# New tables of order, engines and places for a linear-attention and two-MLP kernel

## The chip, the cores and the metric

The kernel runs on one core of a Trainium2 chip. The metric is device time in microseconds (us) of one execution. Five engines work side by side, each through its own queue in order: TensorE (PE, matmuls; PEld are its weight loads), VectorE (DVE), ScalarE (ACT), GpSimd (POOL) and SyncE (SP), which here issues all DMAs. An instruction that waits for another engine holds up everything behind it in its own queue.

## The reference

```python
# attention: batch 4, 8 heads, 576 rows, head_dim 64, 128 features
def phi(x):                      # x scaled by 64 ** -0.25
    proj = np.einsum('bhsd,md->bhsm', x, omega)
    h = proj - np.sum(x * x, axis=-1, keepdims=True) / 2.0
    return np.exp(h - np.max(h, axis=-1, keepdims=True)) / np.sqrt(m)
q_p, k_p = (phi(q_s), phi(k_s))
kv = np.einsum('bhsm,bhsd->bhmd', k_p, v)
num = np.einsum('bhsm,bhmd->bhsd', q_p, kv)
den = np.einsum('bhsm,bhm->bhs', q_p, np.sum(k_p, axis=2))[..., None] + 1e-06
attn = num / den                 # 2304 rows of 512 in all
# first MLP: 512 -> 2048 -> 512
h = np.maximum(x @ w_in, 0.0)
x = h * h @ w_out
# second MLP: rms norm, 512 -> 1536 (gate and value) -> 512
xn = x / np.sqrt(np.mean(x * x, axis=-1, keepdims=True) + 1e-06) * rms_g
g = xn @ w_gate
out = (g / (1.0 + np.exp(-g)) * (xn @ w_val)) @ w_out
```

## The kernel before, in words

The 2304 rows are worked in blocks: 512 rows of each of the four batches, and the 64 remaining rows of all four together as a fifth block of 256. The large matmuls run in float32r, with each operand split into a high part (a cast on ACT, L483) and a low part (a subtraction on DVE or POOL, L474) and three products of the parts. The small matmuls of the attention run in float32. Some block products of the first and second MLP are combined so that seven products replace eight, with sums of operands and results on DVE.

The stages overlap. Attention of a batch goes through pairs of heads. For a pair, PE makes the features of k and of q (L659, a block of 16 matmuls for 512 rows); DVE takes row sums of squares (L613, after a squaring at L580 to L582 on POOL, ACT or DVE), maxima (L666) and two small corrections (L671); ACT takes the exponential (L678); PE transposes (L772) and multiplies (L718, L778, remaining rows at L704, L721, L783); DVE divides (L753 to L757); PE turns the result (L817, L808), and ACT and DVE split it for the first MLP. The first MLP then works hidden unit by hidden unit: a hidden product (L893, 12 matmuls, all in the one PSUM bank of the class "h"), a relu (L908) and a square (L910) on ACT, a low part on DVE or POOL, and four output products of 3 matmuls (L924). The weights are decoded from their input format on DVE and ACT (L512 to L526) and split. The second MLP has products at L1202, sums of results at L1220, gating at L1379 and L1382 and output products at L1398, added up at L1406. In the first 54 us the attention of the first batch is done alone with the first decoded weights; until some 340 us attention is mixed with the first MLP.

Nothing of the order is left to a scheduler while the program is built. Each piece of work is a node with the engines that it may run on and the classes of buffers that it may use. The table ORDER lists all 3753 nodes in the order in which they are issued, and so sets the order in each engine's queue; its top four bits choose among a node's engines. PLACES says which buffer of which class each new buffer takes. The word ffff in ORDER stands for a filler: two matmuls of 256 columns on a tile of ones (L562), whose result nobody reads, issued on PE at that place. The reading of the tables is this:

```python
for w in words:
    if w == 0xFFFF:
        self.filler[1](filled)
        continue
    n = self.nodes[w & 0xFFF]
    n.eng, n.dur, n.fn = n.alts[w >> 12]
```

What a node waits for follows from its data and from the buffer that it takes: a buffer is taken again when its last reader is done.

Of the kernel before, what the change touches and what calls it, by code (L numbers as in the profile page):

```python
# [24 lines left out]
    "0000000400050007001400442045001500461016000300170009ffffffffffffffffffffffffffffffffffff0019000d000a"  # L25
    "0001001a001b0018001c001d00430020100b000c001f001e000e000f0021004f10220010ffffffff00240011002500260008"
    "004e007d001200230050007c00270013ffffffff00470028002affffffffffff0052004800490029004a004b002e002f0180"
    "002b0051002c003000530054004d007e004c0071ffff0080003100550183005601811182005800360037005c0072102d0042"
    "0191007f00810073008200d9003200830184009f00840059105d005a0057018501921193105b00750085005e0186003300da"
    "003400350086003801ae00760077007400640194007800790070005f00b8019501960065003900db1187ffff006000b90066"  # L30
    "006100670068003a00a00069007a003c01a1009e006200a300aa007b008a00ab008701a200a10197006300a41198003e01a4"
    "003b0088003f009201a300a500a200a600a7008c00e401af0089003d00e5008b11b00093013800ae01a510ac00ad0094008d"
    "00af00b000a900e600b100b2008e008f009500a801b100b400b3006b006e00ce00b5009600b600e7009700e80090009100ba"
    "01b201b300d8004000c000b7009901a600bb01be006f006a00bc00c100e900ea00c20041018900eb01a701b400ec00bd00be"
    "00bf009c006c00ee00c311b501c1018a00c400c500c700ca01bf00dd11c0009d00dc012e00cb018b006d00ed01c201c311a8"
    "00de10cf01da018c018d00cd00d000c60098009a01c400c800df00c900e0010400e101caffffffffffff0199019a01cb018e"
    "01cd01c501ce00e2019b019c0410118f01e700d101db11cc01cf0190019d01e811e901dc01dd110501de01b701b801b901df"
    "00d200d3009b01d011d1019e119f01ba01ac01e001a001e101ea01eb0157010f00d401f600d5020301aa00e301d301d401ec"
    "01f901f701ab11f801c600d601fa01ad01fb020401ed01ee010e111001bb21bc00cc01c8112f120502060207020801c70213"
    "01d201fc00f2022f00d701fd010601d501c900ef021f11bd01d601d721d801d901ef01f001f1021410f100f4011101390216"  # L40
    "023000f002170209021500f301b602180219023c01e30220012c01e4020a0200021a013000f50222022301e60102047100f6"
    "00f7020200f90221022400fa01e5023200f8024b011202310233023402250226023d0113011401f2020c020d01f301ff01f4"
    "0235020100fb0115020e113a023f01160240023e02410236011801f50117013b0103047202580107024e024f012d0274020f"
    "02420210010801881211024c02591243021d024d02280229025a025b01090250010a010b022a00fd021c0237021b0212025c"
    "025d025102520473022b0158026802840100010d0101021e0275127602770253025e0278027904061159022c010c02380244"
    "024502460247122d125f023a0285026b0269026c011c011d011e126a0119011a00fc0163026d0239015a0291011b00fe011f"
    "012001210122026e00ff0490122e0123023b116401650286126f027a027b0257013c013d013e02a002540255013f02870288"
    "01400256027c026102890124026201e2029402950292024801420125149124071249024a028a026302641293026501310296"
    "128b02bd02710492029701320133126601340135022702a301360267029801fe0270027d027e027f0141016202a112a2043c"
    "02a4027202a5028f02c002be12bf02c102ad01461148041d028002a612a702e602c2029901370260029a029b0273028e02ae"  # L50
    "02b012af02b102b2029c028102b302e7014302b602c902c312c40147014502b402d912e802b70144028d01a91282141e02ca"
    "02b80405041f0290040802cc02cd0283014902ac035202cb02ce035c014a029d129e02da014d03870156029f02dc02cf12d0"
    "014b014c014e02aa014f035d02db02a902f502ab02b902ba02dd02de12bb143d01660167035102df02c601270168016902d2"
    "02e9016a02ea012a02c502e0035e02d3016b02c702d10302012b02eb02bc02f802f9135302ec12ed015b015c030302f612f7"
    "031202e3015d016c02d4015e02d502fa015f03050306035402c8016004b702e402e202ee02ef02f0031302e102fb13040307"
    "028c035f0161131402f10170043e02b504c602f202e503500308031e02d603930171016d016e016f0368117212fc03090150"
    "015212d701530315031603170369032e030b033b015101540360015503210173030c017401770178017903180175017602d8"
    "030d1394030e0361017b22f3031f030102fe0388017e0362036302ff04b8017f0320136a030004b912f40364036503670355"
    "0322031904ba03230324031a031c030f13100366032f020b133004cb036b031d0331132503920356031b04bb03320357033e"
    "03580327032803290359035a033c02fd0447035b0395133d03330334033f017a037304d703400341017c017d032a032b132c"  # L60
    "030a0588131105861335036c036d036e033a036f037003710589033703740372032604bf03380339134203b204df04c00587"
# [1527 lines left out]
```

## Time and profile before

| | |
|---|---|
| median of 3 runs | 955.78 us (954.9 to 957.16) |
| profiled execution, own time | 957.46 us |
| its span, first to last instruction | 955.2 us |
| mean granted TensorE clock | 0.996 |
| busy: PE, DVE, ACT, POOL | 934.9, 743.2, 515.8, 108.2 us |

The profiled execution is 1.7 us above the median, and 2.3 us of its own time lie outside its span. A matmul's end is modelled in the profile, so PE is shown as busy for somewhat longer than it works; the distance from one matmul's start to the next one's is the better measure. In a dense stretch 12 matmuls of 512 columns take 2.72 us.

### The profile page before, as it was taken

The numbers are of one execution on the slowest core, as the hardware profiler recorded it, in microseconds if no ns is written. First come the engines' busy times: TensorE is split into PE (matmuls) and PEld (weight loads), VectorE is DVE, ScalarE is ACT, GpSimd is POOL, SyncE is SP. The second block draws the span as 40 slices with busy tenths as digits, with TensorE's granted clock in tenths as the row PEclk, the third lists the DMA queues.
The fourth block names the chain that finished last, engine by engine and source line by source line (L and its number), as shares of the span: only waits on it lengthen the run. The fifth ranks groups of instructions, "written<-read, shape, count | busy, mean of one in ns | idle before, by whom it ended". The sixth has DMA issues, their size and how long they took to land.

```text
span 955.2 us, 16357 instructions
## 1 busy us (share of the span) xinstructions
PE 934.9 (98%) x6062; PEld 780.7 (82%) x6062; DVE 743.2 (78%) x1354; ACT 515.8 (54%) x1077; POOL 108.2 (11%) x97
## 2 busy tenths in 40 slices
PE   8899999999999999999999999999999999999998
PEld 7777777878888888888889888888878888888886
DVE  6999999787676798887776778789998746655846
ACT  6888887735665477755345646455443333332321
POOL 2311222120302000010010011001110000101100
PEclk9999999999999999999999999999999999999999
DMA  8657889887978877778788553325232332212203
GB/s 275 222 199 262 286 276 338 292 265 255 325 264 265 276 239 248 239 259 288 243 305 286 196 150 109 113 75 156 77 100 82 100 106 67 67 56 63 72 21 111
DMA packets 78384, 182.10 MB, mean 191 GB/s; under 512 B 9184, under 2 KB 13408, under 8 KB 78304
## 3 DMA queue, kind: packets, MB, share of 16 engines
q1 hardware_dynamic: 78304, 181.06, 58.1%
q8 instruction: 48, 0.79, 0.3%
q14 instruction: 32, 0.26, 0.1%
HBM read 142.49 MB, written 38.54 MB: 190 GB/s over the span
## 4 chain that ended last, share of the span: by engine, by line
PE 79%; DVE 7%; ACT 2%; issue 1%; DMA 1%; SPq 0%; DVEq 0%; ACTq 0%
PE acc L1202 19%; PE t L1398 12%; PE t L1202 8%; PE acc L924 8%; PE h L893 7%; PE acc L1324 5%; PE h L1202 4%; PE t L1324 4%; PE h L1398 3%; PE t L659 2%; PE t L1304 2%; PE h L1304 1%; PE h L1324 1%; PE t L778 1%; DMA wq<-w2d0g 1%
## 5 line engine op out<-in xcount | busy, mean ns | idle before, releaser
L1202 PE MATMUL acc<-x,wq 128*128 128x512 f32 x439 | 153.1, 390 | 0.7 <-DVE cc L1220 0.7
L1202 PE MATMUL acc<-xa,wq 128*128 128x512 f32 x360 | 133.5, 390 | 0.0
L1220 DVE TENSOR_TENSOR cc<-acc,cc 128x512 f32<-128x512 f32 x115 | 78.4, 686 | 50.0 <-PE acc L1202 43.2
L1398 PE MATMUL t<-wq,ub 128*128 128x512 f32 x391 | 105.2, 389 | 0.0
L1202 PEld LDWEIGHTS acc<-x,wq 128*128 128x128 f32 x439 | 82.4, 188 | 18.4 <-DVE cc L1220 1.7
L483 ACT CAST wq<-wq 128x512 fp32r<-128x512 f32 x108 | 64.0, 618 | 60.6 <-DMA wq<-w2d3o 7.8
L474 DVE TENSOR_TENSOR wq<-wq 128x512 fp32r<-128x512 f32 x108 | 79.8, 752 | 17.6 <-ACT wq L483 17.5
L924 PE MATMUL acc<-g,wr 128*128 128x512 f32 (+1 forms) x396 | 91.2, 362 | 0.3 <-DVE g L474 0.2
L1398 PEld LDWEIGHTS t<-wq,ub 128*128 128x128 f32 x391 | 73.1, 188 | 15.1
L1202 PEld LDWEIGHTS acc<-xa,wq 128*128 128x128 f32 x360 | 67.4, 188 | 13.5
L678 ACT ACTIVATE p<-t,sm 128x128 f32<-128x128 f32 x212 | 60.1, 386 | 25.5 <-DVE sm L671 21.6
L924 PEld LDWEIGHTS acc<-g,wr 128*128 128x128 f32 x396 | 64.6, 189 | 11.2 <-issue 0.5
L893 PE MATMUL h<-x,wr 128*128 128x512 f32 x264 | 69.0, 398 | 1.1 <-ACT wr L483 0.5
L1406 DVE TENSOR_TENSOR oa<-t,oa 128x512 f32<-128x512 f32 x73 | 49.3, 684 | 18.6 <-PE t L1398 18.5
L893 PEld LDWEIGHTS h<-x,wr 128*128 128x128 f32 x264 | 48.3, 189 | 12.5 <-ACT wr L483 0.7
L666 DVE TENSOR_REDUCE sm<-t 128x4 f32<-128x512 f32 x59 | 38.5, 684 | 20.2 <-PE t L659 18.4
L521 ACT ACTIVATE dw<-st 128x512 f32<-128x512 f32 x59 | 40.4, 686 | 10.5 <-DMA st<-in_w_gate_dram 3.0
L1398 PE MATMUL t<-wq,g 128*128 128x512 f32 x143 | 45.1, 389 | 0.0
L526 DVE SCALAR_TENSOR_TENSOR dw<-dw,st 128x512 uint32<-128x512 uint32 x59 | 42.0, 715 | 3.1 <-ACT st L515 1.7
L483 ACT CAST ub<-cc 128x512 fp32r<-128x512 f32 x40 | 24.5, 620 | 34.3 <-DVE cc L1382 29.8
L924 PE MATMUL acc<-g,wu 128*128 128x512 f32 (+1 forms) x180 | 42.6, 362 | 0.0
L1202 PEld LDWEIGHTS t<-xq,wq 128*128 128x128 f32 x288 | 37.8, 191 | 2.0
(350 smaller groups left out, 1999.3 us busy)
## 6 DMA issues: line engine op xcount, KB each, us to landing
wr<-w1d SPq DMA_DIRECT2D x70, 512.0 KB, 5.7
st<-in_w_out_dram SPq DMA_DIRECT2D x28, 512.0 KB, 4.5
w1d<-wr SPq DMA_DIRECT2D x22, 512.0 KB, 6.0
st<-in_w_in_dram SPq DMA_DIRECT2D x16, 512.0 KB, 4.9
st<-in_w_gate_dram SPq DMA_DIRECT2D x12, 512.0 KB, 5.3
st<-in_w_val_dram SPq DMA_DIRECT2D x12, 512.0 KB, 5.7
st<-y SPq DMA_DIRECT2D x22, 256.0 KB, 3.7
v<-in_v_r_dram SPq DMA_DIRECT2D x16, 260.0 KB, 4.9
```

Source lines behind the costliest of these rows:

```text
L474: return lambda: en.tensor_tensor(out=lo(), in0=src(), in1=f32(hi()), op=ALU.subtract)
L483: first = plan.add("ACT", act(n), prio, lambda: nc.scalar.copy(out=hi(), in_=src()), rd, [whi], after, pre=[blo] if blo is not bhi else [])
L521: lambda: nc.scalar.activation(out=out(), in_=hf(), func=AF.Abs, scale=65536.0), [(st, 1)], [w])
L526: lambda: nc.vector.scalar_tensor_tensor(out=out().bitcast(U32), in0=out().bitcast(U32), scalar=3, in1=half(st.ap, 0), op0=ALU.logical_shi ...
L678: nc.scalar.activation(out=pbuf.ap[:, j, :], in_=fp.ap[:, i, :], func=AF.Exp, bias=mx.ap[:, j:j + 1])
L893: nc.tensor.matmul(hb.ap[:, :n], lhsT=u.ap[:, wl, kk * P:(kk + 1) * P], rhs=xcols(j, xl, kk)(), start=(gi == 0 and ii == 0), stop=(gi == l ...
L924: nc.tensor.matmul(accs[e].ap[:, :n], lhsT=u.ap[:, w, es], rhs=x.ap[:, :n], start=(c == 0 and i == 0), stop=(c == C1 - 1 and i == 2))
L1202: nc.tensor.matmul(bank.ap[:, cols], lhsT=u.ap[:, wl, c0 + kk * P:c0 + (kk + 1) * P], rhs=x[kk][xl].ap[:, :cols.stop - cols.start], start= ...
L1220: lambda: nc.vector.tensor_tensor(out=out.ap, in0=bank.ap, in1=x.ap, op=ALU.add), [bank, x], [out])
L1324: nc.tensor.matmul(bank.ap, lhsT=us[dc].ap[:, wl, es], rhs=gs[dc, j][xl].ap, start=dc == i == 0 and (j == 1 or first), stop=dc == 1 and i ...
L1398: nc.tensor.matmul(o.ap, lhsT=x[xl].ap[:, c0:c0 + P], rhs=us[f"o{i}"].ap[:, wl, :], start=i == n == 0, stop=i == 1 and n == 2)
L1406: lambda: nc.vector.tensor_tensor(out=oa.ap, in0=o.ap, in1=oa.ap, op=ALU.add), [o, oa], [oa])
```

## The change

Only the numbers of ORDER and PLACES are others; no other line of the program differs, and every line number grows by 2. One line of each table, as an example:

```diff
 ORDER = bytes.fromhex(
-    "0000000400050007001400442045001500461016000300170009ffffffffffffffffffffffffffffffffffff0019000d000a"
...
 PLACES = bytes.fromhex(
-    "4000010001008182004000000202400103040001830101054102020082810202400306000000010483000740008100008201"
...
+    "0000408100000101024082010000020341010283010004050242068182020100030001000783400004080641020001000001"
```

The work is the same, but for these choices: 112 filler matmuls stand in the order in place of 42. POOL has ten more nodes than before (102 in place of 92): eighteen sums of 256 columns at L977 in place of seven, 59 low parts in place of 56, 16 squarings in place of 20. DVE has 13 nodes fewer, ACT 3 more.

The first place is the head of PE's queue: fillers (L562, L564 after) and blocks of features (L659, L661 after). Names: oms is the feature matrix, tr, lt and tt hold the turned rows of the remaining rows, k or q; acc, t and h are PSUM banks. Before:

```order
L562 MATMUL acc_197<-ones 128x256 x18
L659 MATMUL acc_235<-oms,tr_202 128x128
L659 MATMUL acc_236<-oms,tr_202 128x128
...
L659 MATMUL h_246<-oms,lt_215 128x128
L659 MATMUL t_247<-oms,lt_215 128x128
...
L562 MATMUL acc_197<-ones 128x256 x4
L659 MATMUL acc_297<-oms,lt_271 128x128
L659 MATMUL t_298<-oms,lt_271 128x128
```

And after:

```order
L564 MATMUL acc_197<-ones 128x256 x30
L661 MATMUL acc_243<-oms,tr_211 128x128
L661 MATMUL t_244<-oms,tr_211 128x128
...
L564 MATMUL acc_197<-ones 128x256 x14
L661 MATMUL acc_278<-oms,tt_262 128x128
L661 MATMUL t_279<-oms,tt_262 128x128
...
L564 MATMUL acc_197<-ones 128x256 x10
...
L564 MATMUL acc_197<-ones 128x256 x26
```

There are 30, 14, 10 and 26 fillers in front of the first four blocks of features, where 18, 0, 4 and 4 stood.

The second place is DVE's queue where the first weight is decoded (L512, L517, L526; st is the loaded weight, dw the decoded one) between the statistics (sm) of the head pairs. Before:

```order
L512 TENSOR_SCALAR st_384<-st_384 128x512
L517 SCALAR_TENSOR_TENSOR st_384<-st_384 128x512
L576 COPY kv_83<-t_386 128x2x65
L613 TENSOR_REDUCE sm_472<-ld_315 128x8
L666 TENSOR_REDUCE sm_474<-t_431 128x4
L666 TENSOR_REDUCE sm_474<-acc_432 128x4
L671 SCALAR_TENSOR_TENSOR sm_474<-sm_472,sm_474 128x8
```

And after:

```order
L673 SCALAR_TENSOR_TENSOR sm_446<-sm_293,sm_446 128x8
L514 TENSOR_SCALAR st_479<-st_479 128x512
L673 SCALAR_TENSOR_TENSOR sm_446<-sm_293,sm_446 128x8
L519 SCALAR_TENSOR_TENSOR st_479<-st_479 128x512
L578 COPY qr_498<-t_497 128x128
L668 TENSOR_REDUCE sm_530<-acc_513 128x4
```

Instructions that read what the one right in front of them writes now have another one between them here.

The third place is PE's queue between the second and the third hidden product of the first block (wu and wr are weights, x parts of the attention's result). Before:

```order
L893 MATMUL h_1017<-x_942,wu_681 128x512
L893 MATMUL h_1017<-x_941,wu_681 128x512
L659 MATMUL t_1047<-oms,lt_987 128x128
L659 MATMUL t_1048<-oms,lt_987 128x128
...
L893 MATMUL h_1071<-x_727,wr_918 128x512
```

And after:

```order
L895 MATMUL h_1084<-x_1009,wu_749 128x512
L895 MATMUL h_1084<-x_1008,wu_749 128x512
L895 MATMUL h_1128<-x_817,wr_991 128x512
L895 MATMUL h_1128<-x_982,wr_991 128x512
L895 MATMUL h_1128<-x_915,wr_991 128x512
```

The block of features that stood between the two products has moved elsewhere, and the third product follows the second in the same bank.

## Rows read from the trace of the kernel before

**Rows 1.** Page, part 1: busy us (share of the span) and instructions.
```profile
PE 934.9 (98%) x6062; PEld 780.7 (82%) x6062; DVE 743.2 (78%) x1354; ACT 515.8 (54%) x1077; POOL 108.2 (11%) x97
```

**Rows 2.** Windows: length, busy us (instructions) per engine, granted clock, DMA share, GB/s.
```profile
1.00:53.60 52.60, 44.12 (x614) 37.85 (x615) 44.91 (x105) 38.99 (x116) 11.99 (x13) 0.94 0.72 233
53.60:100.00 46.40, 45.12 (x313) 36.05 (x312) 43.36 (x88) 42.76 (x89) 7.82 (x6) 1.00 0.75 250
100.00:340.00 240.00, 236.66 (x2149) 192.13 (x2148) 188.37 (x413) 153.93 (x376) 41.47 (x37) 1.00 0.86 286
340.00:560.00 220.00, 218.19 (x1139) 187.00 (x1138) 174.96 (x304) 126.67 (x227) 10.61 (x12) 1.00 0.75 252
560.00:951.00 391.00, 390.30 (x1854) 327.62 (x1853) 290.79 (x445) 153.47 (x272) 35.82 (x26) 1.00 0.29 86
951.00:955.20 4.20, 0.47 (x3) 0.04 (x1) 0.69 (x1) 0.00 (x0) 0.00 (x0) 0.87 0.52 192
```

**Rows 3.** Timeline of DVE, first 62 us: start, us, operation, count, [idle before].
```profile
8.46 0.69 DVE L613 TENSOR_REDUCE sm<-ld 128x8 f32<-128x512 f32 x1 [1.36 <-ACT ld L581]
...
15.08 1.18 DVE L671 SCALAR_TENSOR_TENSOR sm<-sm,sm 128x8 f32<-128x8 f32 x2
16.18 1.28 DVE L666 TENSOR_REDUCE sm<-acc 128x4 f32<-128x512 f32 x2
...
45.69 2.17 DVE L671 SCALAR_TENSOR_TENSOR sm<-sm,sm 128x8 f32<-128x8 f32 x2
...
57.50 0.42 DVE L512 TENSOR_SCALAR st<-st 128x512 uint32<-128x512 uint32 x1
57.83 0.69 DVE L517 SCALAR_TENSOR_TENSOR st<-st 128x512 uint32<-128x512 uint32 x1
...
59.77 0.42 DVE L512 TENSOR_SCALAR st<-st 128x512 uint32<-128x512 uint32 x1
60.22 0.69 DVE L517 SCALAR_TENSOR_TENSOR st<-st 128x512 uint32<-128x512 uint32 x1
```

**Rows 4.** Timeline of POOL, first 62 us.
```profile
15.19 1.04 POOL L580 TENSOR_TENSOR ld<-ld 128x512 f32<-128x512 f32 x1 [0.95 <-DMA ld<-in_q_r_dram]
...
45.31 2.52 POOL L474 TENSOR_TENSOR wr<-dw,wr 128x512 fp32r<-128x512 f32 x2 [9.31 <-ACT wr L483]
```

**Rows 5.** Timeline of PE, first 16 us.
```profile
1.05 4.21 PE L562 MATMUL acc<-ones 128*128 128x256 f32 x18 [1.05 <-DVE ones L546]
...
8.78 0.58 PE L659 MATMUL h<-oms,lt 64*128 64x128 f32 x1 [2.43 <-DMA lt<-in_k_t_dram]
...
13.06 0.74 PE L562 MATMUL acc<-ones 128*128 128x256 f32 x4
13.73 1.16 PE L659 MATMUL acc<-oms,tt 64*128 64x128 f32 x16
14.82 0.98 PE L562 MATMUL acc<-ones 128*128 128x256 f32 x6
15.73 0.37 PE L659 MATMUL t<-oms,tt 64*128 64x128 f32 x1
```

**Rows 6.** Windows in the head, columns as in the second group.
```profile
5.00:16.00 11.00, 8.57 (x84) 7.23 (x84) 8.48 (x17) 6.16 (x20) 1.85 (x2) 0.84 1.01 322
...
49.60:53.00 3.40, 3.40 (x21) 2.84 (x22) 3.11 (x7) 2.20 (x7) 0.00 (x0) 0.50 0.02 5
```

**Rows 7.** The chain of work, 700 to 715 us: start, us, what.
```profile
709.68 2.87 PE t L1202 x24
```

**Rows 8.** Timeline of PE at its four longest waits behind 60 us.
```profile
82.62 1.16 PE L659 MATMUL t<-oms,lt 64*128 64x128 f32 x16 [0.97 <-PE acc L924]
...
211.27 0.34 PE L808 MATMUL t<-ident,xw 128*64 128x64 f32 x4 [1.62 <-DVE xw L757]
...
516.47 0.74 PE L893 MATMUL h<-xr,wu 128*128 128x256 f32 x4 [0.92 <-ACT f L908]
...
544.86 0.50 PE L1202 MATMUL h<-x,wq 128*128 128x512 f32 x1 [0.66 <-ACT cc L1379]
```

More of the change, by code (lines that the diff above doesn't have):

```diff
@@ L30 @@
[L30 to L44, printed above, removed]
@@ new lines @@
+    "0049004a004b007f0053004d007c0037004c002e102f00540018002b0180018300a0002c102d0055005c0181005600580057"
+    "00801182105d019100710081008201ae10a10059005a00ab009f01840083105b008400860032003301920038003900640185"
+    "00e50065003a003400aa005e009e00cd01a1005fffffffff0075018601af0085119301b01187003b003500760060006100b8"
+    "10b9ffffffffffff008c006600ac00a300770194006200a20063008d0078006710e60079008a007a019500680196008b007b"
+    "00a4009200a500d801a400ad01a20197007001beffffffff00aeffffffffffff008700a600a700af0069119800b011a300b1"
@@ new lines @@
+    "0093008800e401a500b200a901a60089003dffff003c00a8008e008f01b101b2003e003f00b3009400900095009100ce0040"
+    "00b40096009700d900b500b600e801a70099009c00da10b700ba00e700c000bb11a801ca00cc00e900980041ffffffff00bc"
+    "009d00c100c201b300bd01c1006b01bf00c300be01b40189006e00c400bf00c5006f11b5ffffffff00c700ea010400eb00ec"
+    "01c000ca10cf006a00dc00ee006c0162018a018b00cbffff018c018d018e01da01c200dd01c301cb00d001db11dc00de00db"
+    "01c411c500df01cc013800e001cd019900e1019a019b019c01ce01e7118f01cf012d019d006d019e01dd019001e811e900e3"
@@ new lines @@
+    "00ed009a01de01b701b801df0139213a01d001d101b901ba01ab00d100d200d301e011e1119f009b01ea00e201d301eb01ec"
+    "01d401d501f601f901f701ed010200d400d501aa01fa11f801fb0203020401d601ee01d200d700d601ad2105020601a001ac"
+    "01ef020701fc00f2020500f311fd01bb041010f400ef0213021610f000f101c7021402081215021701f001f104710103013b"
+    "021f0218020911bc01bd01f200f500f6022f01c9010e0220020a02191472022100f7010600f801c80222020c01c6021a00f9"
+    "023001d70223022400fa020d11d801d902320231010f111001e501120225023c0158020e024b00fb00fd020b010002330234"
@@ new lines @@
+    "01e402351159023d12260111025801e30490020f01130114015a1236023f01e60201012c011501f30228022901160188024c"
+    "0118024e020211f40240123e02410117022a01ff02420200024f0268124d02500107010111f5027412430108010902511252"
+    "021012110212022b021b0269021c025b02440245026b0246025c010a012e026c010b010d0259010c125a025d021d025e021e"
+    "126a01e2011c0119026d04730275011e00fc111a023a125f022c02760239023b015700fe00ff027704910247023800c6011d"
+    "0278011b022d04920284011f122e0248026102910262026302790120012300c800c901210122026e027a01fe126f013c027b"
@@ L216 @@
+    "060a024006040200004342410609030240030740020202014008404241050107024243400501020003050101400400024001"
+    "00400843024041090100030602400102084301400002000140"
 )
```

338 lines of the change are left out of this document (167 added, 171 removed).

## The prediction

> **What bounds the kernel now.** I read the page first, then a table of windows by stage, then the timelines of single engines in the stages where PE falls short. The page has PE busy for 98% of the span [rows 1], so a new order can win only what PE stands idle or works slowly. The windows say where that is [rows 2]. From 1.0 to 53.6 us PE is busy for 44.1 of 52.6 us, at a mean granted clock of 0.94; from 53.6 to 100 it lacks 1.3 us, from 100 to 340 3.3 us, from 340 to 560 1.8 us and from 560 to 951 0.7 us. The last 4.2 us, behind the last matmul, are one sum on DVE and the store of the last rows; the new order ends with the same pair, so I leave it out. The head is therefore the stage to look at. Its end I take where the first block's first hidden product (L893) is finished, at 53.6 us.
>
> In the head DVE is the engine that the others wait for: busy for 44.9 of 52.6 us [rows 2], and its timeline shows hardly a gap after 8.46 us, where it had waited 1.36 us [rows 3]. Some of what counts as busy there is waiting. A correction of 8 columns (L671) belongs to a pair that takes 0.37 us when undisturbed, but at 15.08 a pair takes 1.18 us, and at 45.69 one takes 2.17 us [rows 3]; POOL runs a two-input operation from 15.19 to 16.23 and two from 45.31 to 47.83 [rows 4], and DVE goes on when POOL's operation ends. The timeline has five such holds in the head, at 15.28, 19.89, 35.30, 45.69 and 46.65, with 0.81, 0.86, 0.56, 0.76 and 1.04 us beyond the usual duration: 4.0 us. A second cost is small and frequent: an L517 that follows its own L512 starts 0.45 us after it (59.77 to 60.22), one that follows another tile's L512 after 0.33 us (57.50 to 57.83) [rows 3]. So a result that is used by the very next instruction costs some 0.12 us more.
>
> **The change part by part.** All terms are differences to the profiled execution (own time 957.46 us, span 955.2 us, 2.3 us around it), whose own time is 1.7 us above the median of 955.78; I apply the sum to the median.
>
> *Neighbours on DVE.* In DVE's queue up to the low part of the fourth piece of the first batch's x (at 51.3 us in this trace), 34 instructions read what the one right before them wrote; in the new order there are 17. At 0.12 us each this is -2.0 us. The other DVE work up to there is nearly the same (one L517 and one L613 fewer, one squaring and three short copies more, within 0.1 us). Bounds: 0, if it is hidden by another wait, and -2.0.
>
> The Trainium skill ("VectorE: DVE Perf Modes", sections "The DRAIN you can't avoid" and "Rules for kernel authors") speaks against this term: every DVE operation pays its flush whether or not the next one depends on it, so that the number of operations is what counts, not their chaining. By that rule the term is zero. The distances 0.45 and 0.33 us of this trace [rows 3] do not agree with it.
>
> *Holds by POOL.* POOL has ten operations in the head before, and five DVE holds came of them; the new order has eight there. At the same rate this gives 4 holds, -0.8 us; without any, -4.0 us. I take -1.5, nearer to the first, since the small pairs of L671 are now more often taken apart and stand between reductions. If the new overlaps are worse (one hold per operation, eight of 0.8 us), it is +2.4.
>
> *Fillers.* Seventy matmuls more on PE, all in the head. At the higher clock one takes 0.12 us (24 of 256 columns in 2.87 us [rows 7]); with the change of data type on both sides, four take 0.67 us (13.06 to 13.73) and six 0.91 us (14.82 to 15.73) [rows 5], which is 0.15 to 0.17 us each, or 0.1 us per change of type. At the lower clock 18 took 4.2 us, 0.23 us each [rows 5]. Their price is what they push back. Up to the fourth block of features, PE's queue after the change is 1.05 us of start, 18 fillers at 0.23, 62 at 0.12, six changes of type and three blocks of 1.09 us (13.73 to 14.82): 1.05 + 4.2 + 7.4 + 0.6 + 3.3 = 16.5 us. Before, the fourth block started at 13.73. But DVE, which waits for it, came to that block's maximum only at 16.18 [rows 3]; after the change the block is done at 17.6, 1.4 us later, and DVE's queue has two more 0.60 us instructions in front of that point. The net loss is 0.2 us. Bounds: -1.6, if DVE's waits in front of 16 us (1.36 us and a short one) go and the fillers hide behind the loads, and +5.7, which is 54 more fillers in front of that block (80 in place of 26) at 0.15 us (8.1) less the 2.4 us that PE is idle between 5 and 16 us [rows 6].
>
> *The clock.* At 49.6 to 53.0 the granted clock is 0.50 (the lower level, 1.2 GHz), right behind a wait of PE, and the window from 5 to 16 us shows 0.84, with another such stretch behind the 2.43 us wait at 8.78 [rows 5, 6]. In the first stretch PE is busy for all 3.4 us, so at the higher level it would have been 1.7 us shorter; but DVE is the later engine there. I put it at 0, with -1.7 as the far end.
>
> *Waits behind the head.* The four longest are 0.97, 1.62, 0.92 and 0.66 us [rows 8]. For three of them the matmul work that stands between the waiting instruction and the one whose result comes back to it through DVE or ACT grows in the new order: 2.0 to 4.5 us for the block at 82.62, 1.4 to 4.0 for L808 at 211.27, 1.1 to 1.8 for L893 at 516.47. I count these as gone, -3.5 us; the one at 544.86 keeps its 1.4 us of work and stays. What comes instead: the third hidden product of the first block now directly follows the second in the same bank, so PE must wait for the relu between. That is the kind of wait that took 0.92 us at 516.47: +0.9. At three more places the new order leaves less than 0.2 us over the copy that PE waits for; 0 to 0.9 us each, I take 0.3: +0.9. Sum -1.7, bounds -4.2 (none of the new ones, and the fourth gone too) and +2.7 (the old ones turn up elsewhere).
>
> *Changes of type.* Leaving the fillers out, PE changes between float32 and float32r blocks 124 times in place of 118, at 0.1 us: +0.6.
>
> *Later load of the engines.* POOL's eleven more sums at L977 are 256 columns each and lie where the second MLP's weights are prepared, between 340 and 560 us, where PE lacks only 1.8 us in 220 [rows 2]. They take work off DVE and can hold it; PE's work runs far enough behind DVE's there that I count nothing.
>
> The sum is -2.0 - 1.5 + 0.2 - 1.7 + 0.6 = -4.4 us, so 955.8 - 4.4 = **951.4 us**.
>
> **The rivals.**
>
> *The fillers cost more than they fill (slower).* If the clock stays at the lower level until the fourth block, as it was in 3.4 us of the stretch from 5 to 16 [rows 6], the 80 fillers in front of that block cost 0.23 us each and the four blocks twice 1.09: 1.05 + 18.4 + 8.7 = 28.2 us until the block is done, 10.6 later than in the forecast. Some 2.4 us of that PE idled before in any case [rows 6], which leaves 8.2. DVE then waits for PE, and the part of its gains that lies in front of that point (about a third of 3.5 us) vanishes as well: -4.4 + 8.2 + 1.2 = +5.0, 960.8 us. It decides at a mean filler price of about 0.17 us over the 62 that I count at the higher clock: 62 x 0.05 + 1.2 = 4.3 us eats the gain. For it: a group of four did cost 0.17 [rows 5]. Against it: the fillers keep PE going, and the two stretches at the lower clock followed waits [rows 5, 6].
>
> *The neighbours cost nothing.* If the 0.12 us belongs to the operations and not to their order, the first term goes: 955.8 - 2.4 = 953.4 us. For it: only one kind of pair is measured here without a neighbour's help. Against it: the same L512 and L517 show both distances within 3 us [rows 3].
>
> *All that is won in the head is given back.* PE's work up to the first hidden product trails DVE's by a little more than before (in the new order the last low part of x comes behind 98 rows of DVE's queue instead of 93), and if the waits behind 60 us only move, what is left is the changes of type and a few tenths: 955.5 us. For it: the windows from 100 to 951 us show PE short by just 5.8 us in all [rows 2]. Against it: three of the four longest waits do get room.
>
> *Everything works.* No holds in the head (-4.0), neighbours (-2.0), one stretch at the lower clock less (-1.7), the waits at their lower bound (-4.2), changes +0.6: -11.3 in full; the first three share one path, on which PE's own queue leaves about 8 us, so I take -10: 945.8 us.
>
> **How the numbers follow.** Chances: my forecast 0.50 (its own range 947.5 to 954.5), fillers too dear 0.16, neighbours free 0.10, given back 0.12, everything works 0.12. The likeliest gives 951.4. The range of 945.0 to 957.5 leaves out most of the slower rival and a little of the best case, together under 0.2. A change of 0.2%, 1.9 us, is about what a measurement of this kernel can tell from none: the bounds are 953.9 and 957.7. Faster: nearly all of the forecast (0.46), most of the neighbours' rival (0.07), all of the best case (0.12), a little of the given back: 0.66. Slower: the filler rival but for its short forms (0.14) and the tail of the given back (0.03): 0.17. Within: 0.17.
>
> **What would show it right or wrong.** In the profile of the changed kernel, the first hidden product should be done near 50.5 us, where it was done at 53.6, with pairs of L673 that take over 0.9 us three or four times in the head at most; the fourth block of features should start at 16 to 17 us; the granted clock should be 0.95 or more over the head. Behind 60 us no wait of over 1 us should stand at L810, and one of 0.7 to 1.0 us at the third hidden product. The prediction is wrong if the first hidden product ends after 53 us, if fillers take over 0.17 us each with the types changed, or if PE's shortfall between 100 and 951 us is above 6 us.

## The result, and the profile after

The changed kernel takes 945.07 us (median of 4 runs, 944.95 to 945.25), the kernel before beside it 955.34 us; the ratio is 0.9893, 95% interval 0.9873 to 0.9913. That is 10.3 us less, where 4.4 were forecast. The profiled execution's span is 943.1 us against 955.2: 12.1 us less, since the one profiled before lay 1.7 us above its median.

The first view is the page's line of busy times. It answers to [rows 1].

```profile
PE 937.4 (99%) x6132; PEld 787.0 (83%) x6132; DVE 726.9 (77%) x1341; ACT 514.8 (55%) x1080; POOL 119.1 (13%) x107
```

PE has 70 matmuls more (the fillers) and no idle time to speak of; DVE is busy for 16 us less, POOL for 11 more. The windows of the changed kernel answer to [rows 2].

```profile
1.00:53.60 52.60, 52.55 (x708) 47.29 (x708) 45.48 (x114) 42.11 (x117) 11.47 (x11) 1.00 0.77 257
53.60:100.00 46.40, 45.71 (x390) 36.96 (x388) 41.84 (x88) 42.24 (x96) 15.01 (x11) 1.00 0.79 256
100.00:220.00 120.00, 120.00 (x1024) 97.45 (x1021) 100.13 (x217) 86.50 (x209) 21.11 (x16) 1.00 0.88 298
220.00:340.00 120.00, 120.00 (x1071) 97.41 (x1069) 84.00 (x195) 78.25 (x182) 15.26 (x16) 1.00 0.82 281
340.00:560.00 220.00, 219.82 (x1147) 189.06 (x1146) 178.26 (x302) 115.60 (x213) 23.90 (x25) 1.00 0.72 244
560.00:940.00 380.00, 379.36 (x1806) 318.82 (x1804) 276.95 (x428) 149.77 (x266) 31.98 (x23) 1.00 0.29 87
```

The window from 100 to 220 us was not shown of the kernel before; there it is:

```profile
100.00:220.00 120.00, 116.80 (x1068) 94.29 (x1068) 104.08 (x216) 84.02 (x203) 24.89 (x20) 1.00 0.89 297
```

Two things are to be seen. PE, which lacked 3.2 us from 100 to 220, lacks nothing, and from 220 to 340 neither. And DVE's third number: with the same count of instructions (88 and 88, 216 and 217) it is busy for 1.5 us less from 53.6 to 100 and for 4.0 us less from 100 to 220. The granted clock is 1.00 in the head, where it was 0.94.

The head, in PE's timeline:

```profile
13.66 3.38 PE L564 MATMUL acc<-ones 128*128 128x256 f32 x26
16.97 1.16 PE L661 MATMUL acc<-oms,tt 64*128 64x128 f32 x16
...
48.98 0.86 PE L895 MATMUL h<-x,wr 128*128 128x512 f32 x3
49.77 1.16 PE L661 MATMUL t<-oms,lt 64*128 64x128 f32 x16
50.86 3.02 PE L895 MATMUL h<-x,wu 128*128 128x512 f32 x12
54.57 3.01 PE L895 MATMUL h<-x,wr 128*128 128x512 f32 x12 [0.69 <-ACT f L910]
```

The fourth block of features starts at 16.97 us; the last group of the first hidden product starts at 48.98, so the product is done at 49.8; the third hidden product waits 0.69 us for the relu of the second. Before, the first hidden product ended later than the 53.6 us that the prediction gives:

```profile
52.60 1.80 PE L893 MATMUL h<-x,wr 128*128 128x512 f32 x6
```

These are its last two groups. The last one starts at 53.56 us, which the prediction took for the end; the product is done at 54.4. From start to start the gain is 4.6 us, where 3.1 were forecast for this landmark.

In DVE's timeline of the head two pairs of L673 are held by POOL for over half a microsecond, where five were [rows 3]. POOL's operations at the same time stand below them:

```profile
13.20 1.24 DVE L673 SCALAR_TENSOR_TENSOR sm<-sm,sm 128x8 f32<-128x8 f32 x2
...
16.27 1.02 DVE L673 SCALAR_TENSOR_TENSOR sm<-sm,sm 128x8 f32<-128x8 f32 x2
```

```profile
13.18 1.04 POOL L582 TENSOR_TENSOR ld<-ld 128x512 f32<-128x512 f32 x1 [11.40 <-DVE sm L668]
16.02 1.04 POOL L582 TENSOR_TENSOR ld<-ld 128x512 f32<-128x512 f32 x1 [1.81 <-DMA ld<-in_q_r_dram]
```

Where the 12.1 us lie can be worked out from the starts of PE's matmuls. Each kind has a usual distance from its start to the next one's (0.227 us for 512 columns, 0.120 for 256, 0.109 for 128, 0.029 for up to 65, 0.0545 for a matmul of a features' block). The time of a stretch less these distances, with fillers counted as nothing, is what PE loses in it. A wait takes more of that than its idle time, 0.17 us in the mean: the profile lets a matmul of 512 columns end 0.39 us after its start, and idle time counts from there, but in a dense row the next one starts 0.23 us after it.

```profile
545.20 0.39 PE L1202 MATMUL h<-xa,wq 128*128 128x512 f32 x1
545.43 0.40 PE L1202 MATMUL h<-x,wq 128*128 128x512 f32 x1
```

The last two columns give the waits with this part included.

| stretch (us) | lost before | lost after | waits of PE with this part, before | after |
|---|---|---|---|---|
| 0 to 54 | 26.6 | 23.6 | fillers and 11 waits | fillers |
| 54 to 100 | 5.1 | 3.4 | 4, 2.0 us | 1, 0.85 us |
| 100 to 220 | 12.9 | 8.8 | 5, 4.1 us | none |
| 220 to 340 | 8.4 | 8.1 | 2, 0.45 us | none |
| 340 to 560 | 3.2 | 1.4 | 3, 2.3 us | 1, 0.3 us |
| 560 to end | 6.1 | 4.9 | 2, 1.0 us | none |
| sum | 62.3 | 50.2 | behind 54 us: 16, 9.9 us | 2, 1.2 us |

So the head brings 3.0 us and the rest 9.1. The forecast had 3.3 in the head and 1.1 behind it.

### The profile page after: what moved, and what is told of

Its sections match the earlier page's. It is cut to its first block, busy times and chain, and to the rows that moved or that the text cites. A ratio compares the mean times of both kernels' runs of the same rounds, so it can differ in the third digit from the quotient of the medians.

```text
span 943.1 us, 16522 instructions
## 1 busy us (share of the span) xinstructions
PE 937.4 (99%) x6132; PEld 787.0 (83%) x6132; DVE 726.9 (77%) x1341; ACT 514.8 (55%) x1080; POOL 119.1 (13%) x107
## 4 chain that ended last, share of the span: by engine, by line
PE 99%; DVE 1%; issue 0%; ACT 0%; DVEq 0%
PE acc L1204 21%; PE acc L926 12%; PE h L895 12%; PE t L1400 12%; PE t L1204 8%; PE acc L1326 5%; PE h L1204 4%; PE h L1400 4%; PE t L661 3%; PE t L1326 3%; PE h L1306 2%; PE acc L564 2%; PE t L720 2%; PE t L1306 1%; PE t L780 1%; PE t L774 1%
## 5 line engine op out<-in xcount | busy, mean ns | idle before, releaser
L1204 PE MATMUL acc<-x,wq 128*128 128x512 f32 x452 | 159.1, 390 | 0.0
L1204 PE MATMUL acc<-xa,wq 128*128 128x512 f32 x350 | 129.7, 389 | 0.0
L1400 PE MATMUL t<-wq,ub 128*128 128x512 f32 x372 | 101.3, 390 | 0.0
L1204 PEld LDWEIGHTS acc<-x,wq 128*128 128x128 f32 x452 | 84.9, 188 | 17.2
L1400 PEld LDWEIGHTS t<-wq,ub 128*128 128x128 f32 x372 | 69.5, 188 | 14.7 <-DVE wq L476 0.4
L476 DVE TENSOR_TENSOR wq<-wq 128x512 fp32r<-128x512 f32 x108 | 75.3, 709 | 4.8 <-ACT wq L485 4.6
L926 PEld LDWEIGHTS acc<-g,wr 128*128 128x128 f32 x396 | 65.0, 189 | 10.5
L1408 DVE TENSOR_TENSOR oa<-t,oa 128x512 f32<-128x512 f32 x67 | 45.2, 683 | 17.4 <-PE t L1400 17.2
L523 ACT ACTIVATE dw<-st 128x512 f32<-128x512 f32 x57 | 39.4, 696 | 15.2 <-DMA w2d4v<-dw 4.5
L1381 ACT ACTIVATE cc<-cc 128x512 f32<-128x512 f32 x36 | 22.3, 628 | 37.5 <-DVE cc L1222 37.5
L910 ACT ACTIVATE f<-h 128x512 f32<-128x512 f32 (+1 forms) x48 | 25.6, 533 | 29.4 <-PE h L895 27.7
L1400 PE MATMUL t<-wq,g 128*128 128x512 f32 x126 | 41.2, 390 | 0.0
```

The lines of the kernel that those rows point to most:

```text
L476: return lambda: en.tensor_tensor(out=lo(), in0=src(), in1=f32(hi()), op=ALU.subtract)
L926: nc.tensor.matmul(accs[e].ap[:, :n], lhsT=u.ap[:, w, es], rhs=x.ap[:, :n], start=(c == 0 and i == 0), stop=(c == C1 - 1 and i == 2))
L1204: nc.tensor.matmul(bank.ap[:, cols], lhsT=u.ap[:, wl, c0 + kk * P:c0 + (kk + 1) * P], rhs=x[kk][xl].ap[:, :cols.stop - cols.start], start= ...
L1400: nc.tensor.matmul(o.ap, lhsT=x[xl].ap[:, c0:c0 + P], rhs=us[f"o{i}"].ap[:, wl, :], start=i == n == 0, stop=i == 1 and n == 2)
L1408: lambda: nc.vector.tensor_tensor(out=oa.ap, in0=o.ap, in1=oa.ap, op=ALU.add), [o, oa], [oa])
```

## The experiments

The kernel before was timed again beside each group of runs (medians 955.3 to 957.9 us), so kernels are compared by their ratio to it; a difference in us is (ratio - 1) x 956. Against this measure the changed kernel stands at -10.2 us (-12.1 to -8.3).

**Fillers and clock.** First the changed kernel with 9 of its 56 filler words (a word, ffff, is two matmuls).

```diff
-0007 0014 ffff x15 0019 ... ffff x7 ... ffff x5 ... ffff x13 ...   (56 in all)
+0007 0014 ffff x9 0019 ...                                         (9 in all)
```

> The changed kernel with the first 18 of its 112 filler matmuls only. Theory A (fillers hold the higher clock, and the clock is worth something on the path): granted clock at the lower level in two or three stretches of the head, first hidden product 2 us later, 1.5 to 3 us above the changed kernel, 946.6 to 948.1. Theory B (DVE sets the pace of the head, the fillers stand where PE would wait): within 0.5 us of the changed kernel, 944.6 to 945.6. Theory C (PE has no wait left in the head because there are more fillers than waits): 1 to 3 us below the changed kernel, 942 to 944.

945.25 us, ratio 0.9877 (0.9859 to 0.9896): no difference from the changed kernel, theory B. Its PE timeline and its window at the lower clock:

```profile
14.26 2.86 PE L659 MATMUL acc<-oms,tt 64*128 64x128 f32 x16 [2.93 <-DMA tt<-in_k_t_dram]
```

```profile
13.43:20.25 6.82, 5.96 (x36) 5.15 (x38) 4.88 (x11) 6.72 (x25) 2.08 (x2) 0.50 0.98 337
```

PE waits for some 7 us in the head again, the clock falls to its lower level (0.50, 1.2 GHz) at 13.43 us, within the wait of 2.93 us, and stays there for 6.8 us, the block takes 2.86 us in place of 1.16, and the time does not move. In the head PE is not the engine that counts. The counterpart is the old order with fillers where PE waited.

```diff
-... 000d ... 00c7 ... 00e8 ...
+... ffff x10 000d ... ffff x9 00c7 ... ffff x5 00e8 ...   (39 words more, 78 matmuls)
```

> The order of the kernel before with 78 filler matmuls more (99 to 120 in place of 42) where PE waited in the head: 20 ahead of the third block of features, 18 ahead of the transposes at L817 and 10 ahead of the block at L659 that waited 1.32 us, the others in twos to sixes. Theory A (the clock is worth something on the path): no lower clock in the head, 1.5 to 2 us below before, 953.3 to 953.8. Theory B (DVE sets the pace): within 0.5 us of before, 954.8 to 955.8. If fillers push back what DVE waits for: 1 to 3 us above before.

Ratio 0.9996 (0.9984 to 1.0009), with a clock of 1.00 over the whole head: theory B again.

**Cuts: one order up to a node, the other behind it.** Buffers whose place was taken get another one.

```diff
-ORDER = after
+ORDER = after[up to node 396] + before[what is left]     (49 us)
```

> The order of the changed kernel up to the last group of the first hidden product (with its 112 filler matmuls), and behind it the order of the kernel before for all that is left; 18 buffers get another place than in either. Theory A (head and rest are two separate gains: work that PE has caught up with by the end of the head is 3.1 us, by the landmark 4.6 us, and the other 7 to 9 us are waits that the new order of the rest removes): 3 to 5 us below before, 950.5 to 952.5. Theory B (the waits behind the head go because DVE leaves the head earlier, whatever the order of the rest): 8 us or more below before, under 947.5. Theory C (a head that is gained is waited away behind it): within 1 us of before, 954.3 to 956.3.

```diff
-ORDER = before
+ORDER = before[up to node 396] + after[what is left]
```

> The order of the kernel before up to the last group of the first hidden product, and behind it the order of the changed kernel for all that is left; 15 buffers get another place, and 19 operations stand later because their place was not free. Theory A: 6 to 9 us below before, 946.5 to 949.5, with fewer than 8 waits of PE over 0.25 us behind the head. Theory B: at most 2 us below before, over 953, with the waits behind the head still there. The prediction's own sizes (waits -1.7, changes of type +0.6): 1.1 us below before, 954.2.

Ratios 0.9996 (0.9983 to 1.0008) and 1.0016 (1.0002 to 1.0031). The new head alone is waited away (theory C), at the seam first (2.54 us) and then at the old places, where 1.62 us became 2.12 [rows 8]:

```profile
62.16 0.96 PE L926 MATMUL acc<-g,wr 128*128 128x512 f32 x3 [2.54 <-DVE xr L476]
...
211.34 0.48 PE L810 MATMUL t<-ident,xw 128*64 128x64 f32 x4 [2.12 <-DVE xw L759]
```

The second is no clean test, since 19 operations were put off and DVE waited 3.1 us for a load of weights at 76 us. Its windows show where it loses:

```profile
53.60:100.00 46.40, 39.68 (x267) 30.99 (x266) 35.23 (x72) 35.12 (x74) 11.16 (x8) 0.93 0.72 228
100.00:220.00 120.00, 119.61 (x1079) 97.19 (x1078) 100.89 (x219) 86.79 (x207) 26.06 (x20) 1.00 0.87 288
220.00:340.00 120.00, 120.00 (x1089) 97.28 (x1088) 82.20 (x193) 78.29 (x191) 15.27 (x16) 1.00 0.82 279
```

PE lacks 6.7 us between 54 and 100 us, behind the seam, and from 100 to 340 us it lacks 0.4: there the new rest is without the old waits behind the old head too. So the cut was made at about 100 us too, where nothing is put off.

```diff
-ORDER = after
+ORDER = after[up to node 287] + before[what is left]     (99 us)
```

> The order of the changed kernel up to the matmuls of node 287 (about 99 us there), behind it that of the kernel before; 12 buffers get another place, nothing stands later. By 100 us the changed kernel has done 4.7 us more matmul work than before and DVE 2.8 to 4.8 us more. Theory D (a lead is only kept by an order that uses it: behind the cut the old order waits again for DVE and for loads, as in the run that was cut at 49 us): 0 to 2 us below before, 953.5 to 956.5. Theory A (gains of the stretches add up): 4 to 6 us below before, 950 to 952.5. Theory B (the lead carries the rest as well): 8 us or more below before.

```diff
-ORDER = before
+ORDER = before[up to node 287] + after[what is left]     (104 us)
```

> The order of the kernel before up to node 287 (104 us there), behind it that of the changed kernel; 7 buffers get another place, nothing stands later (in the cut at 49 us 19 operations did, and a load came 3 us late). From 100 us to the end PE loses 30.6 us against its bare matmul time in the kernel before and 23.2 us in the changed kernel. Theory A: the new rest brings its own 5 to 7 us, 949 to 951.5. Theory D (the new rest lives on the lead of DVE that the new front makes, and waits without it): 0 to 3 us below before, 953 to 956.5, with PE waits of 3 us or more in sum between 100 and 220 us.

Ratios 0.9993 (0.9981 to 1.0005) and 1.0053 (1.0034 to 1.0072). In the first, a lead of 4.3 us at 100 us (31.7 against 27.4 us lost) is gone at the end, 2.7 us of it at the seam:

```profile
104.03 1.16 PE L661 MATMUL t<-oms,lt 64*128 64x128 f32 x16 [2.51 <-issue]
```

The new rest behind the old front is slower than before. DVE there waits long for a result of POOL and for a load, which the old front has not ordered in time:

```profile
109.20 0.69 DVE L613 TENSOR_REDUCE sm<-ld 128x8 f32<-128x512 f32 x1 [6.27 <-POOL ld L580]
...
154.56 0.43 DVE L512 TENSOR_SCALAR st<-st 128x512 uint32<-128x512 uint32 x1 [4.77 <-DMA st<-in_w_in_dram]
```

Theory A, that the stretches add up, has failed for these cuts. A cut mixes two things, though, the order and the misfit at the seam.

**Engines alone.** 221 operations have another engine in the new tables.

```diff
-ORDER word = (engine of after, node)
+ORDER word = (engine of before, node)      in the sequence of after
```

> Order and places of the changed kernel, but each of the 221 operations that changed their engine back on the one it has before (65 subtractions between DVE and POOL, 97 copies and casts between ACT and DVE, 59 others). DVE is busy for 727 us in the changed kernel, 735 before. Theory E (the relief of DVE takes the waits behind the head away): 5 to 9 us above the changed kernel, 950 to 954. Theory O (the order does, engines matter little): 0 to 2 us above it, 945 to 947. Theory I (the tables only work together): above before's 955.

```diff
-ORDER word = (engine of before, node)
+ORDER word = (engine of after, node)       in the sequence of before
```

> Order and places of the kernel before with the engines of the changed kernel at the 221 operations. Theory E: 4 to 8 us below before, 948 to 951. Theory O: within 2 us of before, 954 to 957. Theory I: over 2 us above before.

987.53 us, ratio 1.0326 (1.0299 to 1.0352), and 983.50 us, 1.0293 (1.0270 to 1.0315): theory I. Each order fits its own engines only: with the other's engines it is about 30 us slower than the kernel before, which is three times what the change brings. The new places alone were not tried.

**DVE's neighbours.**

```diff
-DVE queue of the head: 19 operations right behind the one that they read
+DVE queue of the head: 46, by shifting 19 operations
```

> The changed kernel with 19 operations of DVE's queue in the head shifted, so that 46 of them follow directly on the one whose result they read, in place of 19; engines, places and the rest unchanged. If a neighbour costs the 0.12 us that the prediction took and DVE sets the pace of the head: 27 x 0.12 = 3.2 us more in the head, 3 to 4 us above the changed kernel, 948 to 949. If chaining costs nothing (the Trainium skill, VectorE: DVE Perf Modes, The DRAIN you can't avoid): within 0.5 us, 944.6 to 945.6.

```diff
-DVE queue of the head: 19 operations right behind the one that they read
+DVE queue of the head: 2, by pulling 14 operations forward
```

> The changed kernel with 14 operations in DVE's queue of the head pulled forward by one to three places, so that 2 operations follow directly on the one whose result they read, in place of 19. With 27 neighbours more the time rose by 4.8 us, 0.18 us each. Theory N (each neighbour costs DVE that much, and DVE sets the pace of the head): 17 x 0.12 to 0.18 = 2 to 3 us below the changed kernel, 942 to 943. Theory W (the operations put between wait for their loads or for PE instead): 0 to 2 us above it, 945 to 947.

949.84 us, 0.9926 (0.9909 to 0.9943), and 948.39 us, 0.9926 (0.9904 to 0.9947): both slower than the changed kernel, by 3.2 us in the ratios and 4.8 and 3.3 in the medians. The intervals of these ratios overlap that of the changed kernel, but the times themselves do not (at least 947.58 us against at most 945.25). The first lies where the neighbours' price would put it, but DVE also waits for other engines and loads there for 9.6 us in the head in place of 6.5. The second is theory W: DVE loses over 1 us less to neighbours in the head, but waits 11.9 us. So these two do not show the price of a neighbour by themselves. The traces do: over the four of before, after and these two, a TENSOR_SCALAR of the weights' decoding is followed after 0.456 us by an instruction that reads its result (78 pairs) and after 0.335 us by another one (164); a TENSOR_TENSOR of 512 columns after 0.725 (95) and 0.601 us (1159). That is 0.12 us each time.

**DVE late.** A maximum of DVE at 42 us is done five times in the changed kernel and in the one before.

```diff
-            n.fn()
+            for _ in range(5 if n.idx == 234 else 1):
+                n.fn()
```

> The changed kernel with one of DVE's maxima (node 234, at about 42 us) done five times in place of once: DVE is 4 x 0.63 = 2.5 us later from there on. Theory P (in the changed kernel PE sets the pace behind the head and DVE has some us in hand): 0 to 1 us above the changed kernel, 945 to 946. Theory V (DVE sets the pace in both kernels): 2.5 us above the changed kernel, 947.6. If the order only fits the exact times it was made for: more than 2.5 us, over 948.

> The kernel before with the same maximum done five times, DVE 2.5 us later from about 43 us on. Theory V and theory P both have DVE set the pace in the kernel before: 2.5 us above before, 958 to 959. If what PE waits for behind the head are loads or ACT, not DVE: 0 to 1 us above before, 955.5 to 956.5.

948.24 us, 0.9916 (0.9902 to 0.9930), and 1.0022 (1.0010 to 1.0034). Against the changed kernel that is 2.2 us by the ratio and 3.2 by the median, and 2.1 us (1.0 to 3.2) against before: a delay of 2.5 us passes to the end in both, as theory V has it. (The median of the first, 948.24, lies 0.24 us inside the range of the third expectation, an order that fits its exact times only; the ratio does not.) In the head DVE sets the pace in both. But the waits behind the head do not come back. The windows from 100 to 340 us of the new order with its DVE late, with neighbours back, and with fewer neighbours, one each:

```profile
100.00:340.00 240.00, 240.00 (x2122) 195.04 (x2121) 184.43 (x411) 165.07 (x392) 37.07 (x33) 1.00 0.85 289
```

```profile
100.00:340.00 240.00, 240.00 (x2139) 194.89 (x2134) 184.29 (x410) 166.13 (x394) 39.61 (x35) 1.00 0.86 290
```

```profile
100.00:340.00 240.00, 240.00 (x2121) 194.94 (x2120) 184.38 (x410) 166.23 (x395) 38.05 (x34) 1.00 0.84 289
```

PE is busy for 240.00 of 240 us in each of these late versions. In the second and third the gain of the head is gone as well, but for a few tenths at most: up to 54 us PE loses 27.5 and 26.2 us by the measure of the table above, where the kernel before loses 26.6. Still 7.1 of the 10.2 us remain in both. What keeps PE busy behind the head is in the tables of that stretch, not in the lead from the head.

**Are the waits local?** In the old order 13 matmul blocks were pulled in front of six waits; in the new one a block of features was put in front of the third hidden product.

```diff
-... 274 ... 511 513 ...          252 569 571, 326 627 654, 694 653 656, 336 337, 2353 2350 2349 2352 2351
+... 511 513 274 ...              569 571 252, 627 654 326, 653 656 694, 337 336, 2350 2349 2352 2351 2353
```

> The kernel before; ahead of six of PE's waits behind the head (82.6, 102.8, 120.1, 127.6, 153.0 and 516.5 us; 4.5 us with their restarts) one to four matmul blocks are pulled forward that stood behind the waiting one and whose operands are there (13 blocks in all, 0.36 to 0.68 us each). Nothing else changes. Theory L (such a wait is local, it goes with the work put in front of it): 3.5 to 4.5 us below before, about 951.5. Theory P (other engines set the pace, the wait comes back at the next place): within 1 us of before.

```diff
-... 411 412 439 440 441 427 209 ...
+... 411 412 209 439 440 441 427 ...
```

> The changed kernel with one block of features (node 209, 1.09 us, ready long before) put in front of the third hidden product of the first block, where PE waits 0.69 us (0.85 us with the restart). Theory L: the wait goes and nothing comes for it, 0.7 to 0.9 us below the changed kernel, 944.2. Theory P: within 0.3 us of it. If the block's results come too early for DVE's queue or too late for others: up to 1 us above it.

Ratios 1.0008 (0.9991 to 1.0024) and 0.9947 (0.9929 to 0.9965; 951.34 us). The first is theory P: behind 54 us PE still waits 9.6 us by the table's measure (9.9 before), at other places or longer at the next one. Two of these and the one that was not touched:

```profile
86.84 1.25 PE L659 MATMUL t<-oms,tt 64*128 64x128 f32 x16 [1.54 <-DMA tt<-in_k_t_dram]
...
151.51 0.66 PE L817 MATMUL t<-ident,xw 128*128 128x128 f32 x4 [0.54 <-ACT kv L575]
...
209.90 0.34 PE L808 MATMUL t<-ident,xw 128*64 128x64 f32 x4 [1.61 <-DVE xw L757]
```

The second was a miss, outside all three expectations: I had called the block ready, but it had to wait 3.96 us for ACT. The time is 5.2 us above the changed kernel by the ratios and 6.3 by the medians; behind the wait the granted clock is at its lower level as well (0.93 in the mean from 53.6 to 100 us).

```profile
57.69 2.08 PE L661 MATMUL t<-oms,tt 64*128 64x128 f32 x16 [3.96 <-ACT p L680]
```

**DVE's load.** Less of it in the old order, more in the new one.

```diff
-                lambda: nc.vector.tensor_reduce(out=ss.ap[:, :8], in_=x.ap, op=ALU.add, axis=AX), [x], [ss],
+                lambda: nc.vector.tensor_reduce(out=ss.ap[:, :8], in_=x.ap[:, :, :8] if short else x.ap,
+                                                op=ALU.add, axis=AX), [x], [ss],
```

> The kernel before; the 25 sums of squares at L613 behind the head read 8 of each 64 columns, so that each takes about 0.13 in place of 0.68 us and DVE has some 13 us less to do between 54 and 290 us (the rest of the sums is left out). If DVE's work sets the pace that makes PE wait behind the head: the waits of PE between 54 and 340 us (6.5 us with their restarts) mostly go, 4 to 7 us below before, 949 to 952. If loads or the order of the queues set it: 0 to 1.5 us below before, 954 to 956.

```diff
-            n.fn()
+            for _ in range(2 if n.idx in (317, 306, 359, 348, 866, 854, 877) else 1):
+                n.fn()
```

> The changed kernel with seven of DVE's maxima between 103 and 205 us done twice: 7 x 0.60 = 4.2 us more work for DVE, as much as it has more in the kernel before between 100 and 220 us (104.1 against 100.1). Theory L (the lower load of DVE is what removes PE's waits there): the waits come back, 3 to 5 us above the changed kernel, 948 to 950. Theory R (the arrangement does, DVE has some us in hand): no wait of PE between 100 and 220 us, 0 to 1 us above it, 945 to 946.

The first: 953.53 us, 0.9967 (0.9949 to 0.9984), 3.2 us less than before; its medians differ by 4.4. It lies between the two expectations: each sum still took 0.21 us in place of 0.68, so DVE had some 12 us less to do (25 x 0.47), and a quarter of that came out. The second: 948.46 us, 0.9915 (0.9894 to 0.9936). By the medians that is 3.4 us above the changed kernel, by the ratios 2.1, and the intervals of the two overlap; the trace decides. Its window and its longest wait from 100 to 220 us:

```profile
100.00:220.00 120.00, 117.84 (x1009) 94.46 (x1005) 100.95 (x219) 83.74 (x201) 20.96 (x16) 1.00 0.86 290
```

```profile
192.71 0.69 PE L781 MATMUL t<-kv,qt 128*64 128x65 f32 x16 [1.08 <-DVE xr L477]
```

PE has six waits there again, 3.3 us by the table's measure, where the old order has 4.1 and the new one none, and the span is 4.2 us longer. Giving DVE back the load that it had lost in this stretch brings most of the waits back (theory L).

**Cuts at the end of attention.**

```diff
-ORDER = after
+ORDER = after[up to node 1524] + before[what is left]     (324 us)
```

> The order of the changed kernel up to node 1524 (324 us there), behind it the order of the kernel before; 5 buffers get another place, nothing stands later. By 340 us the new order has won 9.1 of its 12.1 us against the profiled execution. If the gain of head and middle together is kept by the old rest: 6 to 9 us below before, 947 to 950. If it is given back there as behind the cuts at 49 and 100 us: 0 to 2 us below before.

```diff
-ORDER = before
+ORDER = before[up to node 1540] + after[what is left]     (344 us)
```

> The order of the kernel before up to node 1540 (344 us there), behind it the order of the changed kernel; 8 buffers get another place, nothing stands later. If the last stretch brings its own part (3.1 us by the profiles, of which 2 us are waits at 516, 536 and 545 us): 2 to 3 us below before, 953 to 954. If only the whole plan brings it: within 1 us of before, or above it.

950.91 us, 0.9942 (0.9922 to 0.9961), so 5.5 us of the gain are kept; at the seam PE waits 2.1 us (1.87 of them at 337.67 for a result of DVE), and behind 340 us some of the old waits are back, 1.7 us. The other cut: 1.0000 (0.9986 to 1.0013). The last stretch alone brings nothing: two new waits for DVE and ACT, 1.32 us at 351.6 and 0.63 us at 354.3, eat what it saves. So at least 5.5 of the 10.2 us are made up to 324 us, by the new front and the new middle together; the last stretch adds nothing unless it stands behind these.

No version tried is faster than the changed kernel; the one with 94 fillers fewer is as fast.

## Why the prediction was wrong

The sign and the head were right, and the size was wrong: the time lies outside the range given for the forecast itself, 947.5 to 954.5 us. The step that failed is "Waits behind the head", -1.7 us, which measured -8.7 (9.9 to 1.2 us), and with it its mechanism, since it looked at PE's queue and left out the holds of DVE behind the head.

- *Waits behind the head.* I took the four longest, three of them gone (-3.5), and added 1.8 for new ones. In the trace the fourth went too (-0.7), twelve shorter ones went with them (-2.9), the new ones were 0.9 in all (-0.9), and each wait costs some 0.17 us beyond its idle time, which I had not counted: 16 waits have 7.1 us of idle time and 9.9 us of lost distance (-2.5). That makes -8.7.
- *Why they went.* I explained them by PE's own queue, as the matmul work that stands between an instruction and the result it waits for. The run with six waits eased falls against that: PE's order alone moves such waits and does not remove them. What I left out was DVE behind the head. My two terms for DVE, neighbours and holds, were counted to the end of the head and no further, without a reason. Worked out from the distance between DVE's starts, less the usual one for its kind with an independent instruction behind it (waits for other engines left out), DVE loses some 8.4 us in the head before and 4.9 after, which is the -3.5 that was forecast (-2.0 and -1.5); from 54 to 220 us it loses some 20 us before and 14 after. These 6 us are holds: between 54 and 220 us DVE has 14 instructions that take over 0.25 us longer than usual before, 12.5 us in all, and nine after, 6.6 us, and during each of them a two-input operation of POOL runs. Two of those before, with POOL's operations (L523 takes 0.42 us when undisturbed):

```profile
70.15 1.52 DVE L523 TENSOR_SCALAR dw<-dw 128x512 f32<-128x512 f32 x1
...
122.05 1.52 DVE L523 TENSOR_SCALAR dw<-dw 128x512 f32<-128x512 f32 x1
```

```profile
69.70 1.68 POOL L474 TENSOR_TENSOR g<-f,g 128x512 fp32r<-128x512 f32 x1 [6.50 <-DVE f L582]
...
121.80 1.49 POOL L474 TENSOR_TENSOR wr<-dw,wr 128x512 fp32r<-128x512 f32 x1 [7.53 <-ACT wr L483]
```

  The dependent neighbours there cost about the same in both, some 7 us. That DVE's load matters there is shown by the run that gives 4.2 us of it back. That the arrangement matters as well is shown by the old order with 12 us less load, which wins only 3.2. The two were not told apart further, and no run took the holds alone away, so their share of the -8.7 stays open.
- *Neighbours* and *holds.* Right in size in the head by the trace; the two runs on neighbours do not separate their price at the end. The rule of the Trainium skill that I weighed there (VectorE: DVE Perf Modes, Rules for kernel authors: the flush comes regardless, so the count of operations is what matters) does not agree with the trace in one respect: by the same count, a dependent follower costs 0.12 us in over 170 pairs here.
- *Fillers*, +0.2, and *clock*, 0. Right: the fourth block starts at 16.97 us for 16.5, and taking 94 fillers out, with 6.8 us at the lower clock, changes nothing.
- *Changes of type*, +0.6. Of the right sign and too small: the loss at changes of PE's line from 54 to 340 us went from 10.2 to 11.4 us, 1.2 more.
- *Later load of the engines*, counted as nothing. PE lost 3.0 us less behind 340 us, as much as its waits there fell (3.3 to 0.3), so it is counted above; the last cut shows that it is no term of its own.
- *The sum.* The forecast added a head and a rest. Spliced, they don't add: the new front gives 0 with the old rest behind it, the new rest +5.1 us behind the old front, both up to 324 us -5.5, all of it -10.2. Part of that is the misfit at the seams, which was not separated. Inside the new tables they do add, as far as two runs show: with the head's gain taken out by DVE's queue there, 7.1 us are left. Waits, head and changes of line make -10.5 of the 12.1 us between the two profiled executions; the other 1.6 were not assigned.
- *Two figures* of the prediction do not follow from their own entries. "All is given back" with +0.6 for the changes and a few tenths off would be some 956 us and not 955.5; and if the old waits only move, the new ones alone give +1.8 to +3.6 and not +2.7.
- *The rivals.* The time of "everything works" came (945.8 for 945.07) by luck, and not by its route: two holds stayed, the clock gave nothing, and the waits went well beyond its lower bound of -4.2. "Fillers cost more" fell with the run that takes fillers out, "neighbours cost nothing" by the 0.12 us in the traces. "All is given back" is what happens where the old rest stands behind the new head; the new rest keeps the gain.

Of what I had said would show it, the first hidden product (49.8 us for 50.5), the fourth block, the clock, two holds, no wait over 1 us at L810 and 0.69 us at the third hidden product came as described. The shortfall of PE behind 100 us, which was to stay under 6 us, fell to 0.8.

## What to carry to other kernels

Where an engine sets the pace beyond the stage with the visible stalls, count its small costs (dependent neighbours, holds by another engine) over the whole stretch in which it does so, and read the waits of the engine behind it as their result. Count every wait, the short ones too and what each costs beyond the idle time shown, and not the longest few. Parts of two planned orders can't be priced by splicing them: ask first whether the other engines' queues and loads still fit at the seam.

## What the runs showed of the hardware

- A DVE instruction that reads the result of the one right in front of it starts 0.12 us later than an independent one, in each of the three frequent kinds (0.456 and 0.335 us; 0.725 and 0.601; 0.721 and 0.609).
- A DVE instruction can take 0.25 to 1.1 us longer than usual while a two-input operation of POOL runs: it was so in all 31 long ones of the two kernels between 6 and 220 us (19 before, 12 after).
- A wait of PE costs 0.17 us beyond the idle time that the profile shows (9.9 and 7.1 us in 16 waits), about the 0.16 us by which a matmul's end in the profile lies behind the usual start of the next.
- PE at the lower clock for 6.8 us in the head cost nothing measurable, because DVE was the later engine. The Trainium skill (TensorE: Matmul & The Clock Gate, section Terms, the entry on the time that the throttle is active) puts the penalty at about that time multiplied by the share of the clock that is missing, here 3.4 us as an estimate; 945.25 against 945.07 us shows that this does not reach the time where PE is not on the path.
